# Low halves of the later first-layer weight tiles on VectorE and GpSimd, with the planner's costs and offsets set anew, in a fused attention and feed-forward kernel

## Chip, cores and metric

The kernel runs on one core of a Trainium2 chip. A time is the device time of one execution in microseconds (us), and lower is better. The profile is of one execution of its own.

## What is computed

Block-sparse attention over 4 batches, 8 heads, 768 positions and head size 64, then a feed-forward layer with a leaky activation over all 3072 tokens:

```python
scores = scale * np.matmul(q, k.transpose(0, 1, 3, 2))
...
scores = np.where(mask, scores, -1000000000.0)
scores = scores - np.max(scores, axis=-1, keepdims=True)
attn = np.exp(scores)
attn = attn / (np.sum(attn, axis=-1, keepdims=True) + 1e-09)
return np.matmul(attn, v).astype(np.float32)
...
h = x @ w_in            # x: 3072 x 512, w_in: 512 x 2048
g = np.maximum(h, 0.0) + alpha * np.minimum(h, 0.0)
return (g @ w_out).astype(np.float32)
```

The two weight matrices arrive in eight bytes a number.

## The kernel before, in words

**Split numbers.** Every matmul runs in 16 bit. A number is split into a high part, which is the number scaled by a power of two and rounded to 16 bit, and a low part, which is what the rounding left out, and a product takes three matmuls: high with high, high with low, low with high. `times` makes a high part. `rest` makes a low part, with one instruction on VectorE (DVE in the rows), and with two on GpSimd (POOL): a scaling (L443) and a subtraction (L444).

**Attention.** There are 48 units (a batch, a group of 256 query rows, a pair of heads) of four steps, 192 steps in all. Two steps share one group of eight score matmuls (L653, L659). Per step VectorE adds the mask (`emit_bias`, L669), ScalarE (ACT) takes the exponential (L676), a reciprocal follows (L687), then the high part on ScalarE, GpSimd or VectorE and the low part on VectorE or GpSimd. A DMA from SyncE's queue transposes the pair (`pt<-ph`). When a unit's four steps are there, 36 matmuls multiply by v (L730), and `x` is made, its high part by ScalarE (L741) and its low part by VectorE (L746).

**Feed-forward.** Four units make a chunk of 256 tokens, 12 chunks in all. Per chunk there are eight ups (`emit_up`, 24 matmuls, L1149) and eight downs (`emit_down`, 12 matmuls, L1191). Between up and down, VectorE makes `g` in two instructions (L1159, L1160), ScalarE its high part (L1165) and GpSimd its low part (`emit_gl`, L1170). In a chunk the downs run two ups behind.

**Weights.** There are 16 tiles of `w_in` (`wi` in the rows) and 16 of `w_out` (`wo`), each 512 columns on 128 partitions. After its load a tile goes through three integer steps (L930, L935 or L940, L946), a matmul that finds its scale (`emit_gram`), a high part (`times`), and a low part. For all 16 `wi` tiles and the first 8 `wo` tiles, the low part goes through TensorE (PE): a scaled identity `sid` is made on GpSimd (L1022 or L1026), one 32-bit matmul of the tile with `sid` (L1033, two rows in the trace) and one 16-bit matmul that takes the high part away (L1034) leave the low part in PSUM, and ScalarE copies it to its place (L1038). The last 8 `wo` tiles have their low part made by `rest` on VectorE. The first up stands behind the last scale (`emit_gsc`) in the order.

**What sets the order.** `Plan.run` works through all operations once, before the program is built. It keeps a clock and the queue of each engine; an operation has a priority, a table of engines with a cost on each (`alts`), the operations it needs and the buffers it takes. The constants at the head of the file (`V_WA`, `OFF`, `PREF`, `MOE_LAG`, `MOE_BOOST` and others) set priorities and how dear each engine counts. The result is one fixed order of instructions on each engine, and on the chip each engine goes through its own in that order.

```python
o = plan.op(p + 0.1 + OFF["wh"], {"ACT": 0.63, "DVE": (0.42, 0), "POOL": 0.75}, lambda e, y=y: emit_w_hi(e, "wi", y), [gs[-1], prev])
db = plan.buf("o")
o = plan.op(p - 2 + OFF["wl"], {"PE": 1.2}, lambda y=y, db=db: emit_w_lo_pe("wi", y, db), [o, o_sid], [db], [sb])
prev = o_wi[y] = plan.op(p + OFF["wc"], {"ACT": 0.5}, lambda y=y: emit_w_lo_copy("wi", y), [o], [], [db])
```

## Time and profile before

| | |
|---|---|
| three runs | 816.24, 816.78, 818.37 us, median 816.78 us |
| the profiled execution | 818.19 us, of which the span from the first to the last instruction is 816.5 us |
| busy, share of the span | TensorE 96%, weight loads 62%, VectorE 74%, ScalarE 71%, GpSimd 53% |
| instructions | 16929 |
| DMA | 135.35 MB, mean 166 GB/s |
| first up starts | 115.15 us after the start of the span |

A table of busy shares is a mean over stages. In the span cut into 40 slices the first five look unlike the rest, so the profile is read in two stretches, before and behind the first up. A chain of waits says what the end waited for, and a table of waits in a stretch says what an engine waited for there.

### The profile page before, as it was taken

To read this page: it belongs to the slowest core of one execution; us is meant where nothing else is said; L and a number is where in the kernel's file an instruction comes from. 1 tells how busy PE (TensorE), PEld (TensorE's weight loads), DVE (VectorE), ACT (ScalarE), POOL (GpSimd) and SP (SyncE) were. 2 spreads that over 40 slices of the span, in tenths; PEclk is the share of its full clock that TensorE was granted. 3 is DMA by queue.
4 is the path that set the end of the run, shared out by engine and by line. 5 is a ranking of instruction groups with operands and counts; after the bars stand their busy time and mean duration, and the time that the engine had idled before them with its cause. 6 is when DMAs were issued, how large, how long until landed. Compare 5 with 4: busy or idle time off the path is not lost.

```text
span 816.5 us, 16929 instructions
## 1 busy us (share of the span) xinstructions
PE 781.6 (96%) x6335; PEld 504.1 (62%) x6335; DVE 604.9 (74%) x1279; ACT 576.0 (71%) x1041; POOL 429.9 (53%) x360
## 2 busy tenths in 40 slices
PE   6848899999999999999999999999999999999997
PEld 4423365766766666666666666666666666676764
DVE  6898998887689777797687787958687888734231
ACT  6888997897577778876677878736587888724111
POOL 6475786575336555644355655544265656624121
PEclk9978999999999999999999999999999999999999
DMA  9997996987985979879787979629686887643000
GB/s 331 325 310 208 191 184 146 205 161 162 220 193 122 169 162 194 183 153 199 160 174 142 183 179 209 136 77 193 154 204 157 171 171 151 115 97 84 28 1 26
DMA packets 384722, 135.35 MB, mean 166 GB/s; under 512 B 349028, under 2 KB 377728, under 8 KB 384640
## 3 DMA queue, kind: packets, MB, share of 16 engines
q1 hardware_dynamic: 384576, 134.26, 74.8%
q8 instruction: 49, 0.80, 0.4%
q14 instruction: 33, 0.27, 0.1%
q0 software_dynamic: 64, 0.02, 0.0%
HBM read 35.67 MB, written 6.29 MB: 51 GB/s over the span
## 4 chain that ended last, share of the span: by engine, by line
PE 87%; DVE 4%; ACT 3%; POOL 2%; issue 1%; DMA 1%; POOLq 0%; ACTq 0%; DVEq 0%
PE h L1149 30%; PE o L1191 29%; PE sp L730 12%; PE sp L653 7%; PE sp L659 5%; PE d L1033 3%; ACT wo L935 1%; DVE e L669 1%; DMA kf<-in_k_dram 1%; PE d L1034 1%; POOL ph L444 1%; DVE n L930 1%; PE gram L956 0%; DVE ph L441 0%; POOL e L443 0%
## 5 line engine op out<-in xcount | busy, mean ns | idle before, releaser
L1149 PE MATMUL h<-x,wi 128*128 128x256 f16 x2304 | 267.2, 273 | 0.0
L1149 PEld LDWEIGHTS <-wi 128*128 128x128 f16 x2304 | 222.1, 98 | 46.9 <-issue 10.1
L1170 POOL TENSOR_TENSOR gl<-g,gh 128x512 f16<-128x512 f32 x96 | 115.7, 1205 | 220.3 <-ACT gh L1165 192.2
L1191 PE MATMUL o<-wo,gh 128*128 128x512 f16 x768 | 228.9, 380 | 0.0
L669 DVE CUSTOM_DVE_ANT_0 e<-sp,bias,cs 128x768 f32<-128x768 f32 x192 | 191.2, 1010 | 34.7 <-PE sp L659 16.6
L676 ACT ACTIVATE e<-e,nm 128x768 f32<-128x768 f32 x192 | 177.4, 925 | 18.6 <-DVE nm L669 18.4
L444 POOL TENSOR_TENSOR ph<-e,ph 128x768 f16<-128x768 f32 x96 | 171.6, 1788 | 8.0
L433 ACT ACTIVATE ph<-e,rs 128x768 f16<-128x768 f32 x181 | 164.4, 926 | 10.2 <-DVE rs L687 4.9
L443 POOL TENSOR_SCALAR e<-e,rs 128x768 f32<-128x768 f32 x96 | 92.4, 962 | 112.4 <-ACT ph L433 104.9
L1165 ACT CAST gh<-g 128x512 f16<-128x512 f32 x96 | 59.1, 616 | 125.6 <-DVE g L1160 106.0
L1191 PE MATMUL o<-wo,gl 128*128 128x512 f16 x384 | 145.5, 379 | 0.3 <-POOL gl L1170 0.3
L1159 DVE SCALAR_TENSOR_TENSOR g<-h,am 128x512 f32<-128x512 f32 x96 | 66.1, 689 | 78.3 <-PE h L1149 72.2
L1191 PEld LDWEIGHTS <-gh 128*128 128x128 f16 x768 | 70.5, 98 | 82.2 <-issue 6.3
L441 DVE SCALAR_TENSOR_TENSOR ph<-e,rs,ph 128x768 f16<-128x768 f32 x96 | 111.8, 1164 | 8.9 <-ACT ph L433 8.8
L730 PE MATMUL sp<-pt,v 128*64 128x256 f16 x1728 | 103.5, 274 | 0.0
L730 PEld LDWEIGHTS <-v 128*64 128x64 f16 x1728 | 90.6, 110 | 15.7 <-issue 15.0
L1160 DVE SCALAR_TENSOR_TENSOR g<-h,gsc,g 128x512 f32<-128x512 f32 x96 | 72.1, 751 | 3.4
L1191 PEld LDWEIGHTS <-gl 128*128 128x128 f16 x384 | 37.5, 98 | 46.0 <-POOL gl L1170 0.8
L653 PEld LDWEIGHTS <-qt 128*128 128x128 f16 x384 | 37.6, 98 | 29.3 <-issue 7.5
L653 PE MATMUL sp<-kt,qt 128*128 128x512 f16 x192 | 47.5, 330 | 3.6 <-DVE nm L669 3.6
L741 ACT ACTIVATE x<-sp 128x256 f16<-128x256 f32 x48 | 18.3, 380 | 43.6 <-DVE nm L669 25.1
L659 PE MATMUL sp<-kt,qt 64*128 64x512 f16 x192 | 48.2, 332 | 0.0
(152 smaller groups left out, 725.7 us busy)
## 6 DMA issues: line engine op xcount, KB each, us to landing
wo<-in_moe_w_in_dram SPq DMA_DIRECT2D x16, 512.0 KB, 6.4
raw<-in_moe_w_out_dram SPq DMA_DIRECT2D x16, 512.0 KB, 6.6
kf<-in_k_dram SPq DMA_DIRECT2D x16, 384.0 KB, 3.9
qf<-in_q_dram SPq DMA_DIRECT2D x12, 512.0 KB, 4.8
vf<-in_v_dram SPq DMA_DIRECT2D x16, 384.0 KB, 5.3
out_dram<-ob SPq DMA_DIRECT2D x24, 256.0 KB, 2.3
ks<-kt SPq DMA_DIRECT2D x28, 192.0 KB, 3.3
pt<-ph SPq DMA_TRANSPOSE x192, 3.5
```

Source lines behind the costliest of these rows:

```text
L433: nc.scalar.activation(dst, src, AF.Copy, scale=scale)
L441: nc.vector.scalar_tensor_tensor(dst, src, scale, hi, ALU.mult, ALU.subtract)
L443: nc.gpsimd.tensor_scalar(tmp, src, scale, 1.0, ALU.mult, ALU.mult)
L444: nc.gpsimd.tensor_tensor(dst, tmp, hi, ALU.subtract)
L653: nc.tensor.matmul(T["sp", n + i][:, a:z], T["qt", u][:, h, i, :], (ks, kt)[i][:, h, a:z], start=True, stop=False)
L659: nc.tensor.matmul(T["sp", n + i][:, a:z], T["qt", u][r, h, i, :], (kt, ks)[i][r, h, a:z], start=False, stop=True)
L669: nc.vector.tensor_tensor_reduce(T["e", n], T["sp", n], bias[:, t0 + j % w, :], scale=T["cs", c][:, hp : hp + 1], scalar=3.0e38, op0=ALU.a ...
L676: nc.scalar.activation(T["e", n], T["e", n], AF.Exp, bias=T["nm", n], scale=-1.0, accum_out=T["su", n])
L730: nc.tensor.matmul(av[h * D : (h + 1) * D, : n * P], v2[:, h, t, vv, :], T["pt", u, h][:, pl * NT + t, :], start=(m == 0), stop=(m == len( ...
L1149: nc.tensor.matmul(ph[:, i, :], win(w, f, ct), x[:, ct, :], start=(m == 0), stop=(m == len(terms) - 1))
L1170: nc.gpsimd.tensor_tensor(T["gl", c, j], T["g", c, j], T["gh", c, j], ALU.subtract)
L1191: nc.tensor.matmul(T["o", c][t], g[:, i, t * P : (t + 1) * P], wout(w, f), start=(i == 0 and m == 0 and j in first_j), stop=(i == 1 and m ...
```

## The change

Of the 16 `wi` tiles, tiles 8 to 15 no longer have their low part made through TensorE. They use `rest`, on VectorE or GpSimd as the planner picks, and no `sid` is made for them. The last 8 `wo` tiles may now use GpSimd as well. Softmax steps before step 22 may all use either engine for the low part (`PL0`), where before every second one was held to VectorE. `pa` (a buffer unused here) is no longer kept apart. All other lines change the planner's costs, its offsets, and the time after which it takes a DMA to have been issued.

```diff
-MOE_LAG = 17.620982
+MOE_LAG = 10.557759
-MOE_BOOST = 22.980404
+MOE_BOOST = 59.091694
...
-PL0 = "dv"
+PL0 = "d"
...
+WI_PE = 8
...
-    MAX4 = {"DVE": (0.55, 0), "ACT": 0.88, "POOL": 0.95}
-    LOW4 = {"DVE": (0.94, 0), "POOL": (1.1, 1.7)}
+    MAX4 = {"DVE": (0.55, 0), "ACT": 0.88, "POOL": 0.92}
+    LOW4 = {"DVE": (0.96, 0), "POOL": (0.94, 1.52)}
+    LOWW = {"DVE": (0.67, 0), "POOL": (0.75, 1.24)}
...
         for g in (2 * x, 2 * x + 1):
             sb = plan.buf("sid")
-            o_sid = plan.op(p + OFF["wh"], {"POOL": 0.5}, lambda g=g: emit_sid(g), [gs[-1]], [sb])
+            if 2 * g < WI_PE:
+                o_sid = plan.op(p + OFF["wh"], {"POOL": 0.41}, lambda g=g: emit_sid(g), [gs[-1]], [sb])
             for y in (2 * g, 2 * g + 1):
...
+                if y >= WI_PE:
+                    prev = o_wi[y] = plan.op(p + OFF["wc"], LOWW, lambda e, y=y: emit_w_lo(e, "wi", y), [o])
+                    continue
                 db = plan.buf("o")
...
-            o_wo[y] = plan.op(p - 3 + 0.1 * (y % HF) + OFF["oh"], {"DVE": (0.67, 0)}, lambda e, y=y: emit_w_lo(e, "wo", y), [o])
+            o_wo[y] = plan.op(p - 3 + 0.1 * (y % HF) + OFF["oh"], LOWW, lambda e, y=y: emit_w_lo(e, "wo", y), [o])
```

Lines of the program behind the change are numbered two higher in the helpers and six higher in the feed-forward part. What the change moves is seen at two places.

**TensorE, just ahead of the first up.** `v` is the value tile of attention, `d` the PSUM tile of a weight tile's low part, `h` the result of an up. Before:

```order
L730 LDWEIGHTS v_710
L730 MATMUL sp_74<-pt,v_710 64x256
L1033 MATMUL d<-wi,sid 128x512
L1034 LDWEIGHTS wi
L1034 MATMUL d<-wi 128x512
L1149 LDWEIGHTS wi
L1149 MATMUL h<-x,wi 128x256
```

Of the change:

```order
L732 LDWEIGHTS v_858
L732 MATMUL sp_74<-pt,v_858 64x256
L1155 LDWEIGHTS wi
L1155 MATMUL h<-x,wi 128x256
L1155 LDWEIGHTS wi
```

The low part between the product with v and the first up is gone. Ahead of the first up stand in both orders 11 groups of scores, 4 products with v, the low parts of 8 `wo` tiles, and the low parts of 14 `wi` tiles before and of 8 in the change. Behind it stand the low parts of 2 `wi` tiles before and of none in the change; scores, products, ups and downs are the same in number.

**GpSimd, up to the first low part of `g`** (`gl`), which the first down waits for. `e` and `ph` belong to one softmax step, `qn` to the queries. Before:

```order
L1022 TENSOR_SCALAR sid_1418<-wi_75,ssc_117 128x128
L437 TENSOR_SCALAR wi_75<-wi_75,ssc_117 128x512
L443 TENSOR_SCALAR e_1360<-e_1360,rs_1395 128x768
L444 TENSOR_TENSOR ph_1416<-e_1360,ph_1416 128x768
L437 TENSOR_SCALAR wi_75<-wi_75,ssc_117 128x512
L437 TENSOR_SCALAR qn_1531<-qf_1365,sq_1517 128x8x2x64
L437 TENSOR_SCALAR wo_76<-wo_76,swo_125 128x512
L437 TENSOR_SCALAR ph_1588<-e_1479,rs_1555 128x768
L1170 TENSOR_TENSOR gl_1596<-g_1538,gh_1559 128x512
```

Of the change:

```order
L444 TENSOR_SCALAR wi_75<-wi_75,ssc_117 128x512
L445 TENSOR_TENSOR wi_75<-wi_75 128x512
L444 TENSOR_SCALAR e_1234<-e_1234,rs_1340 128x768
L445 TENSOR_TENSOR ph_1363<-e_1234,ph_1363 128x768
L444 TENSOR_SCALAR e_1326<-e_1326,rs_1373 128x768
L445 TENSOR_TENSOR ph_1389<-e_1326,ph_1389 128x768
L444 TENSOR_SCALAR wi_75<-wi_75,ssc_117 128x512
L445 TENSOR_TENSOR wi_75<-wi_75 128x512
L1176 TENSOR_TENSOR gl_1565<-g_1536,gh_1548 128x512
```

Scalings of single tiles have given way to pairs of a scaling and a subtraction. Four of the five weight tiles that GpSimd takes over, and 15 softmax low parts where there were 10, stand ahead of the first `gl`; the fifth stands between the second `gl` and the third. The three tiles that VectorE takes over stand on it behind the first up.

## Rows read from the trace of the kernel before

**Rows 1.** The page: its span, TensorE's line of the busy times, its line in the 40 slices (tenths busy), and the chain of waits that ended last, by engine.

```profile
span 816.5 us, 16929 instructions
PE 781.6 (96%) x6335; PEld 504.1 (62%) x6335; DVE 604.9 (74%) x1279; ACT 576.0 (71%) x1041; POOL 429.9 (53%) x360
PE   6848899999999999999999999999999999999997
PE 87%; DVE 4%; ACT 3%; POOL 2%; issue 1%; DMA 1%; POOLq 0%; ACTq 0%; DVEq 0%
```

**Rows 2.** Stretches of the span, from and to in us: length, busy us and instructions of each engine, TensorE's granted clock as a share of full speed, DMA share, GB/s. The cuts are GpSimd's first softmax low part, its first `gl`, and the first up.

```profile
0.00:38.30 38.30, 26.73 (x184) 16.43 (x186) 28.22 (x71) 27.68 (x35) 19.51 (x36) 0.96 1.04 324
38.30:121.10 82.80, 64.20 (x457) 34.09 (x454) 76.76 (x173) 75.15 (x130) 59.79 (x56) 0.88 0.97 232
0.00:115.15 115.15, 84.98 (x595) 46.38 (x595) 99.10 (x231) 96.89 (x151) 74.49 (x88) 0.90 0.99 265
115.15:816.50 701.35, 696.59 (x5742) 457.69 (x5740) 505.76 (x1049) 479.08 (x891) 355.45 (x273) 1.00 0.71 149
```

**Rows 3.** TensorE in order of time around the first up: start, length, line, output and inputs, shape, count.

```profile
113.97 1.12 PE L1033 MATMUL d<-wi,sid 128*128 128x512 f32 x2
...
115.15 2.78 PE L1149 MATMUL h<-x,wi 128*128 128x256 f16 x24
117.77 1.02 PE L1033 MATMUL d<-wi,sid 128*128 128x512 f32 x2
...
118.85 0.49 PE L653 MATMUL sp<-ks,qt 128*128 128x512 f16 x2
...
120.02 2.79 PE L1149 MATMUL h<-x,wi 128*128 128x256 f16 x24
122.65 1.02 PE L1033 MATMUL d<-wi,sid 128*128 128x512 f32 x2
...
123.73 0.49 PE L653 MATMUL sp<-ks,qt 128*128 128x512 f16 x2
```

**Rows 4.** Waits of TensorE's matmuls between the first up and 812.2 us, all of them: what waited, for what, us in total, how often, the longest.

```profile
PE o L1191 <- POOL gl L1170: 0.3, 1, 0.3
```

**Rows 5.** VectorE's instructions from the start to 121.2 us, some groups: line, operation, output and inputs, shape, count, busy us, mean ns of one, idle us before them and what ended it.

```profile
L669 DVE CUSTOM_DVE_ANT_0 e<-sp,bias,cs 128x768 f32<-128x768 f32 x23 | 23.2, 1010 | 3.2 <-PE sp L659 2.9 <-POOL ph L444 0.2
L441 DVE SCALAR_TENSOR_TENSOR ph<-e,rs,ph 128x768 f16<-128x768 f32 x10 | 10.7, 1072 | 0.1
L441 DVE SCALAR_TENSOR_TENSOR qn<-qf,sq,qn 128x512 f16<-128x512 f32 x5 | 4.2, 844 | 0.0
L940 DVE SCALAR_TENSOR_TENSOR n<-wo,n 128x512 int32<-128x512 int32 x4 | 2.7, 687 | 0.0
L435 DVE TENSOR_SCALAR v<-vf,sv 128x768 f16<-128x768 f32 x1 | 2.1, 2058 | 0.0
L441 DVE SCALAR_TENSOR_TENSOR kn<-kf,ks,kn 128x768 f16<-128x768 f32 x2 | 2.0, 1018 | 0.1
L963 DVE TENSOR_REDUCE isum<-gram 128x2 bf16<-128x256 f32 x4 | 1.7, 422 | 1.9 <-PE gram L956 1.8
L441 DVE SCALAR_TENSOR_TENSOR v<-vf,sv,v 128x768 f16<-128x768 f32 x1 | 1.7, 1655 | 0.0
L435 DVE TENSOR_SCALAR wo<-wo,swo 128x512 f16<-128x512 f32 x1 | 0.9, 892 | 0.0
L435 DVE TENSOR_SCALAR kn<-kf,ks 128x768 f16<-128x768 f32 x1 | 0.6, 620 | 0.0
L585 DVE COPY kt<-kp 128x768 f16<-128x768 f16 x1 | 0.6, 557 | 1.6 <-PE kp L574 1.6
L600 DVE COPY qt<-qp 128x512 f16<-128x512 f16 x1 | 0.4, 418 | 0.0
```

**Rows 6.** The same view for GpSimd.

```profile
L444 POOL TENSOR_TENSOR ph<-e,ph 128x768 f16<-128x768 f32 x10 | 17.1, 1707 | 0.8
L443 POOL TENSOR_SCALAR e<-e,rs 128x768 f32<-128x768 f32 x10 | 10.6, 1061 | 3.8 <-ACT ph L433 3.5
L437 POOL TENSOR_SCALAR ph<-e,rs 128x768 f16<-128x768 f32 x10 | 10.3, 1027 | 9.2 <-DVE rs L687 5.5 <-ACT dn L681 3.6
L437 POOL TENSOR_SCALAR wi<-wi,ssc 128x512 f16<-128x512 f32 x12 | 8.3, 694 | 9.5 <-PE d L1033 9.5
L444 POOL TENSOR_TENSOR v<-vf,v 128x768 f16<-128x768 f32 x3 | 4.9, 1648 | 0.3
L1022 POOL TENSOR_SCALAR sid<-wi,ssc 128x128 f32<-128x128 f32 x8 | 3.6, 456 | 7.8 <-PE d L1033 6.7 <-DVE ssc L424 1.0
L443 POOL TENSOR_SCALAR vf<-vf,sv 128x768 f32<-128x768 f32 x3 | 3.4, 1141 | 0.1
L437 POOL TENSOR_SCALAR qn<-qf,sq 128x1024 f16<-128x1024 f32 x1 | 1.6, 1552 | 1.1 <-DVE sq L424 1.1
L1170 POOL TENSOR_TENSOR gl<-g,gh 128x512 f16<-128x512 f32 x1 | 1.2, 1162 | 0.0
```

**Rows 7.** GpSimd in order of time: its first softmax low part, with the idle time ahead of it in brackets.

```profile
38.31 0.91 POOL L443 TENSOR_SCALAR e<-e,rs 128x768 f32<-128x768 f32 x1 [1.11 <-ACT ph L433]
39.31 1.65 POOL L444 TENSOR_TENSOR ph<-e,ph 128x768 f16<-128x768 f32 x1
```

More of the change, by code (lines that the diff above doesn't have):

```diff
@@ L27 @@
 SIZES0 = [2, 2, 2]
-MOE_LAG = 17.620982
+MOE_LAG = 10.557759
 EARLY = 15.72
-MOE_BOOST = 22.980404
-V_WA = -4.856569
-W_WA = 1.529176
-V_WB = 4.173325
-W_WB = 1.958978
-LDP = 19.4088
-PL_V = -11.034327
-P_V = 11.063658
+MOE_BOOST = 59.091694
+V_WA = -14.628893
+W_WA = 0.831846
+V_WB = -1.945082
+W_WB = 0.837098
+LDP = 9.849482
+PL_V = -30.458749
+P_V = 70.421934
 PL = "gv"
 NS0 = 22
-PL0 = "dv"
+PL0 = "d"
 LD = 6
@@ L47 @@
 LEADL = 2
-PREF = {"PE": 1.0, "DVE": 3.833567, "ACT": 1.034769, "POOL": 4.794428, "SP": 1.0}
-PREF0 = {"PE": 1.0, "DVE": 1.289575, "ACT": 0.2, "POOL": 0.2, "SP": 1.0}
-SLOW = 1.12
+PREF = {"PE": 1.0, "DVE": 5.665188, "ACT": 1.195828, "POOL": 9.828706, "SP": 1.0}
+PREF0 = {"PE": 1.0, "DVE": 1.638921, "ACT": 0.697709, "POOL": 0.2, "SP": 1.0}
+SLOW = 1.02
 UNTIL = 130.0
 SWITCH = 0.095
-JOIN = 59.615954
-OFF = {"k": -16.711194, "q": -6.049735, "s": -54.854228, "e": 27.549339, "p": -20.301281, "wg": -11.57007, "wh": 69.70885, "wl": -10.883701, "wc": 1.583105, "og": -6.200565, "oh": -4.877295, "ol": 49.769926, "t": 0.0}
-P_AV = 16.415788
+JOIN = 107.16054
+OFF = {"k": -29.572996, "q": -7.007518, "s": -43.09448, "e": 92.848819, "p": -2.021726, "wg": -59.516007, "wh": 83.953384, "wl": -13.645392, "wc": 7.750212, "og": -27.344996, "oh": 18.271827, "ol": 4.243761, "t": 0.0}
+P_AV = 11.44285
 Q_PE = 1
+WI_PE = 8
 N_PS = 6.0
@@ L63 @@
 M_PR = 0.0
-BUFS = {"wr": 4, "vf": 4, "qf": 1, "qt": 3, "qn": 1, "ph": 4, "e": 4, "pt": 4, "x": 2, "junk": 1, "sid": 2, "pa": 1, "kt": 4, "ks": 4, "v2": 4, "gh": 3, "gl": 3}
+BUFS = {"wr": 4, "vf": 4, "qf": 1, "qt": 3, "qn": 1, "ph": 4, "e": 4, "pt": 4, "x": 2, "junk": 1, "sid": 2, "kt": 4, "ks": 4, "v2": 4, "gh": 3, "gl": 3}
 class Buf:
@@ L72, with __init__ @@
 class Op:
-    def __init__(self, n, prio, alts, fn, deps, alloc, use, dma, mode, clear):
-        self.clear = clear
+    def __init__(self, n, prio, alts, fn, deps, alloc, use, dma, mode, clear, lead):
+        self.clear, self.lead = clear, lead
         self.n, self.prio, self.alts, self.fn, self.dma, self.mode = n, prio, alts, fn, dma, mode
@@ L95, in buf, with op @@
         return Buf(pools)
-    def op(self, prio, alts, fn, deps=(), alloc=(), use=(), dma=None, mode=(0, 0), clear=()):
-        o = Op(len(self.ops), prio, alts, fn, deps, list(alloc), list(use), dma, mode, clear)
+    def op(self, prio, alts, fn, deps=(), alloc=(), use=(), dma=None, mode=(0, 0), clear=(), lead=None):
+        o = Op(len(self.ops), prio, alts, fn, deps, list(alloc), list(use), dma, mode, clear, lead)
         for b in o.alloc + o.use:
@@ L210, in run @@
                     if o.dma is not None:
-                        events.append((now + c + 1.0, o.n, "dma", o))
+                        events.append((now + (c + 1.0 if o.lead is None else o.lead), o.n, "dma", o))
                     else:
@@ L860, in attend @@
         hi = plan.op(at("p") - 1, MAX4, lambda e: emit_p_hi(e, n), [o], [pb], [eb])
-        lo = LOW4 if path == "d" else {"POOL": (1.1, 1.7)} if path in "gG" else {"DVE": (0.94, 0)}
+        lo = LOW4 if path == "d" else {"POOL": LOW4["POOL"]} if path in "gG" else {"DVE": LOW4["DVE"]}
         lo = plan.op(at("p") - 1, lo, lambda e: emit_p_lo(e, n), [hi], [], [pb, eb])
         if path in "gvd":
-            o_pt[n] = [plan.op(n - 1, {"SP": 1.7}, lambda: emit_p_t(n), [lo], [ptbuf[u, h]], [pb], dma=1.75)]
+            o_pt[n] = [plan.op(n - 1, {"SP": 1.46}, lambda: emit_p_t(n), [lo], [ptbuf[u, h]], [pb], dma=1.75, lead=0.8)]
             return
@@ L1120, in prep_wo @@
         for y in range(x * HF, (x + 1) * HF):
-            o = plan.op(p - 3 + 0.1 * (y % HF) + OFF["oh"], {"ACT": 0.63, "DVE": (0.42, 0), "POOL": 0.75}, lambda e, y=y: emit_w_hi(e, "wo", y), [o_swo[x], o_wo.get(y - 1)])
+            o = plan.op(p - 3 + 0.1 * (y % HF) + OFF["oh"], {"ACT": 0.68, "DVE": (0.42, 0), "POOL": 0.62}, lambda e, y=y: emit_w_hi(e, "wo", y), [o_swo[x], o_wo.get(y - 1)])
             if WO_PE > x:
@@ L1242, in moe @@
         downs, pas = [], []
-        obufs, pbufs = None, [plan.buf("pa") for _ in range(n)] if half else []
+        obufs, pbufs = None, [plan.buf("vf") for _ in range(n)] if half else []
         for i, (kind, j) in enumerate(items):
```

22 lines of the change are left out of this document (11 added, 11 removed).

## Prediction

> **What bounds the kernel.** I read the page first. TensorE is busy for 96% of the span, the chain of waits that ended last is TensorE for 87%, and the slices show it at 9 from the sixth to the last but one, with fuller engines only ahead of that [rows 1]. A mean over such a span hides two stages, so I then cut it into stretches [rows 2]. Behind the first up, at 115.15 us, TensorE is busy for 696.59 of 701.35 us at the full clock, and the table of waits has one wait of its matmuls in all that time, 0.3 us on GpSimd's `gl` [rows 4]. There the time is the sum of TensorE's work and no other engine counts, so long as it keeps up. Ahead of the first up TensorE is busy for only 84.98 of 115.15 us [rows 2]; VectorE is busy for 99.10 and ScalarE for 96.89, and the DMA engines' share is 0.99. Nobody is alone the bound there. VectorE is nearest, and every step of softmax and every weight tile passes through it.
>
> So the time is the start of the first up plus what TensorE has to do behind it. The order has the same scores, products, ups and downs behind the first up in both versions, down to the same last run of ups and downs. The question is when the first up starts, and whether anything makes TensorE wait soon after.
>
> **Term 1: TensorE's work behind the first up.** Two low parts of `wi` tiles go. One takes 1.08 us from its start to that of what follows (117.77 to 118.85 and 122.65 to 123.73) [rows 3]. The gain is 2 x 1.08 = 2.2 us, all of it on the path. With it the stretch of 701.3 us becomes 699.1. The six other low parts that go stand ahead of the first up, where TensorE idles for 30 us anyway; I count nothing for them. Their cover is VectorE's queue. If TensorE were what the first up waits for, they would give another 6 x 1.18 = 7.1 us [rows 3].
>
> **Term 2: the start of the first up.** The low part of `x` (L746) that completes the first chunk's input is the last thing VectorE owes the first up, so I compare what stands on VectorE up to there, with means from its rows [rows 5]. Less: five softmax low parts (5 x 1.07 = 5.4), two low parts of q (2 x 0.84 = 1.7), one mask step (1.1 with its accumulator), two copies of transposed tiles (0.56 + 0.42), one scaling of v against one low part of v (2.06 - 1.66 = 0.4). More: three integer steps (3 x 0.69 = 2.1), three softmax high parts (as the scaling of k, 3 x 0.62 = 1.9), one weight scaling more on balance (0.89) and four tiny ones (0.6). That is 9.6 less and 5.5 more, a gain of 4.1 us. The three `wi` low parts on VectorE come behind the first up, where it is busy for 505.76 of 701.35 us [rows 2], and cost nothing. ScalarE loses five copies from PSUM, five softmax high parts and three integer steps ahead of the first up and gains a handful of copies, so it has more room. Loads and transposes are the same in number on SyncE's queue, in another order; their share of 0.99 [rows 2] is a rival below.
>
> VectorE idles for 115.15 - 99.10 = 16.05 us ahead of the first up. If it idles as long again, the first up starts at 115.15 - 4.1 = 111.05 us. It could idle less: 2.9 us for scores, 1.8 for the scale sums and 1.6 for a copy that leaves it were waits for TensorE [rows 5], 6.3 us in all. That is the lower end, 104.75 us. The upper end is 115.15 us, nothing gained.
>
> **Term 3: GpSimd, and the first down.** The work that VectorE and ScalarE lose goes to GpSimd. Up to the first `gl` it has [rows 6]: five softmax low parts more (5 x (1.06 + 1.71) = 13.8), two softmax high parts (2.1), one scaling of q (1.6), four low parts of weight tiles and two of q; and less: seven weight scalings (7 x 0.69 = 4.9), four `sid` (1.8), one low part of v (2.8). No row has a low part 512 wide on GpSimd. Its two instructions are bounded below by the scaling of a tile and `gl`, the same widths, 0.69 + 1.16 = 1.86 us, and above by the pair 768 wide, 2.77 us. I take 1.86, since work here goes with width (0.69 against 1.03 us for scalings): 6 x 1.86 = 11.2. The sum is 28.7 - 9.5 = 19.2 us more.
>
> Before, GpSimd works 19.51 + 59.79 = 79.3 us until its first `gl`, and 98.5 us now. Its first softmax low part starts at 38.31 us [rows 7], with 19.5 us done by then. If that is so again, 79.0 us are left and the first `gl` starts at 117.3 at the earliest and ends at 118.5 us. TensorE comes to the first down three ups and one group of scores behind the first up, 2.62 + 2.63 + 2.63 + 1.17 = 9.05 us [rows 3], at 120.1 us. GpSimd may idle for 1.6 us in 79 without harm. Before it idled for 23 us in that stretch; many of those waits were for `sid` and scalings whose tiles TensorE still held (9.5 + 6.7 us in all [rows 6]) and mostly go. The waits for softmax, 5.5 + 3.6 + 3.5 = 12.6 us [rows 6], came to a queue that ran ahead of its inputs; it now runs behind them. I take 3 us of idleness, a quarter, since fewer arrivals should be late for a fuller queue, and keep 0 and 12.6 as ends. The first down then waits 3.0 - 1.6 = 1.4 us. The second `gl` is one softmax low part later, 2.77 + 1.16 us, while TensorE needs over 5 us to the second down, so no more waits follow.
>
> **The sum.** -2.2 - 4.1 + 1.4 = -4.9 us. The profiled execution took 818.19 us for a span of 816.5, so it would take 813.3. It is 1.4 us above the median of the runs; from 816.78 I get **811.9 us**. The ends: with a first up at 104.75 and GpSimd never idle, the first down still waits for the `gl` that ends at 118.5, as if the first up were at 109.45. That is -2.2 - 5.7 = -7.9, or 808.9. If GpSimd's scalings also keep to the 0.91 us of a single one [rows 7], 27 of them save about 4 us more, 805.
>
> **Rivals.**
>
> *The start gives more (0.20).* VectorE's waits for TensorE shrink, and GpSimd is never late: 805 to 809 us, by the ends above. For it: TensorE loses six low parts and ScalarE much work ahead of the first up. Against: GpSimd caps it.
>
> *The start gives nothing (0.17).* The first up waits for the stream of loads and transposes (DMA share 0.99 [rows 2]) or for ScalarE's chain, and starts at 115.15 again. Only term 1 is left: 816.78 - 2.2 = 814.6 us. Against: no group of VectorE's rows has a DMA as the end of its waits [rows 5].
>
> *GpSimd becomes the bound (0.10, slower).* If all 12.6 us of softmax waits stay, its first `gl` ends at 131.1 and the first down waits 11.0 us: -2.2 - 4.1 + 11.0 = +4.7, 821.5 us. It decides at the first down: from a wait of 6.3 us on the change loses. For it: GpSimd has to be busy for 79 of some 80 us, where it was busy for 59.79 of 82.80 [rows 2].
>
> *VectorE and GpSimd stand in each other's way (0.07, slower).* The scaling of v on VectorE took 2.06 us, that of k, the same shape, 0.62; the low part of v took 1.66 and that of k 1.02 [rows 5]. On GpSimd softmax scalings average 1.06 where a single one takes 0.91 [rows 6, 7]. VectorE has 16 scalings and low parts between tiles in SBUF ahead of the first up. If each is stretched by the 0.64 us of the low part of v, the first up starts 10.2 us later, at 121.3, and the time is 816.78 - 2.2 - 4.1 + 10.2 = 820.7 us. Against: the ten softmax low parts average 1.07, hardly over 1.02 [rows 5]. [...]
>
> That the change does not do what it says is ruled out by the order: the eight low parts are gone from TensorE.
>
> **How the numbers follow.** My forecast has 0.46, at 809 to 814 us. A change within 0.3% (2.4 us) can't be told from none, so faster means below 814.3 and slower above 819.2. Faster holds the forecast and the first rival, and a little of the second: 0.68. Same holds most of the second and the weak ends of the slower two: 0.18. Slower: 0.14. The range leaves out the slower cases' upper parts and the best of the first rival: 804.5 to 819.
>
> **What would show it.** Right: the first up near 111 us, 88 to 98 us of GpSimd's work done by its first `gl`, the stretch behind the first up near 699 to 701 us with one wait of 1 to 2 us at the first down. Wrong: a wait for `gl` of over 6 us or a first up behind 115 us (the slower cases), or TensorE waits spread over the later chunks, which would mean that the new offsets starve it and term 1's stretch is not the same work at the same pace.

## The result and the profile after

The changed kernel takes 821.91 us (median of six runs, 819.91 to 823.54) against 816.59 for the kernel before. The ratio is 1.0057, with a 95% interval from 1.0045 to 1.007: slower by 5 us. The prediction said 811.9 (804.5 to 819.0), faster. It was wrong in sign. The profiled execution took 823.54 us for a span of 821.8, 5.3 us more than the 816.5 of [rows 1]; both profiled executions, 823.54 and 818.19 us, stand 1.6 us above their medians.

A line of the page, as in [rows 1]:

```profile
PE 776.4 (94%) x6311; PEld 502.7 (61%) x6311; DVE 609.6 (74%) x1267; ACT 574.0 (70%) x1046; POOL 453.4 (55%) x374
```

TensorE's busy time is 5.2 us shorter than before, yet the span is 5.3 us longer: its idle time grew by 10.5 us. Stretches of the span: ahead of the first up and behind it as in [rows 2], up to GpSimd's first `gl`, from 95 to 130 and to 400 us, and two short ones (length, busy us of PE, weight loads, VectorE, ScalarE and GpSimd, granted clock, DMA share, GB/s):

```profile
0.00:112.12 112.12, 79.28 (x577) 43.94 (x577) 95.56 (x221) 86.37 (x137) 87.55 (x98) 0.82 0.98 268
112.12:821.80 709.68, 697.10 (x5737) 458.73 (x5735) 514.07 (x1047) 487.58 (x911) 365.88 (x277) 1.00 0.72 148
0.00:122.27 122.27, 86.36 (x636) 49.36 (x637) 105.50 (x242) 92.67 (x149) 96.20 (x105) 0.83 0.96 254
95.00:130.00 35.00, 28.44 (x257) 19.00 (x257) 32.41 (x72) 27.83 (x55) 31.07 (x29) 0.95 0.64 130
130.00:400.00 270.00, 264.55 (x2199) 172.64 (x2194) 218.58 (x437) 209.88 (x399) 148.43 (x109) 0.99 0.86 174
104.20:107.40 3.20, 3.20 (x34) 2.50 (x29) 1.85 (x7) 1.85 (x4) 2.92 (x4) 0.50 1.06 232
172.50:175.70 3.20, 3.20 (x33) 2.69 (x29) 0.00 (x0) 0.00 (x0) 1.39 (x2) 0.50 1.10 246
```

The same two stretches of the kernel before:

```profile
95.00:130.00 35.00, 33.72 (x285) 20.44 (x283) 31.97 (x80) 31.70 (x61) 28.04 (x26) 1.00 0.88 172
130.00:400.00 270.00, 270.00 (x2261) 177.95 (x2260) 212.69 (x447) 208.09 (x390) 141.84 (x108) 1.00 0.86 178
```

Length less busy time is TensorE's idle time: from 95 to 400 us 1.28 us before, 6.56 + 5.45 after, 10.7 more. What TensorE waited for behind 100 us in the changed kernel (us in total, how often, the longest); [rows 4], which begins at the first up, has a single 0.3, and 8.4 of the 11.9 us here stand behind the first up:

```profile
PE sp L655 <- DVE nm L671: 4.2, 3, 2.8
PE sp L732 <- DMA pt<-ph: 3.1, 2, 2.4
PE h L1155 <- ACT x L743: 2.3, 1, 2.3
PE sp L655 <- DVE uq L422: 0.9, 1, 0.9
PE h L1155 <- DVE x L748: 0.7, 1, 0.7
PE otot L977 <- DVE osum L965: 0.7, 1, 0.7
```

Most of it is softmax and `x`: scores wait for VectorE's mask step (`nm`), products for the transposed softmax parts (`pt`), ups for `x`. TensorE in order of time around the first up (L1155), and at 172 us:

```profile
102.74 0.49 PE L655 MATMUL sp<-kt,qt 128*128 128x512 f16 x2 [2.80 <-DVE nm L671]
...
103.58 3.58 PE L732 MATMUL sp<-pt,v 128*64 128x256 f16 x36
...
110.03 2.16 PE L732 MATMUL sp<-pt,v 128*64 128x256 f16 x36
112.12 0.50 PE L1155 MATMUL h<-x,wi 128*128 128x256 f16 x3
114.94 0.60 PE L1155 MATMUL h<-x,wi 128*128 128x256 f16 x4 [2.32 <-ACT x L743]
116.28 4.64 PE L1155 MATMUL h<-x,wi 128*128 128x256 f16 x41 [0.74 <-DVE x L748]
...
172.17 3.82 PE L732 MATMUL sp<-pt,v 128*64 128x256 f16 x35 [2.35 <-DMA pt<-ph]
```

Two things are to be seen. The first up starts at 112.12 us, near the forecast, but runs three matmuls and then waits 2.32 + 0.74 us for `x`; 17 of its 24 matmuls run from 116.28 us on, so it ends about where it did before. And the 36 matmuls of a product take 2.16 us, but 3.58 and (35 of them) 3.82 us behind a wait of 2.8 and of 2.35 us. The two short stretches above show why: the granted clock is 0.50 there, where the kernel before has 1.00 from 95 to 400 us. That costs 1.4 + 1.7 = 3.1 us more. The sum closes: 10.7 of waits, 3.1 of clock, less eight low parts of 1.08 us [rows 3], is +5.2 us against a measured +5.3.

It also shows where the change loses. From 130 to 400 us it idles for 5.45 us (3.1 for `pt`, 1.4 for `nm`, 0.9 for a scale of the queries, `uq`), where the kernel before is busy for 270.00 of 270, and one product there costs 1.7 us more at the half clock. These 7.2 us are more than the whole loss of 5.3: at 130 us the changed kernel was still about 1.9 us ahead.

### The profile page after: what moved, and what is told of

It is laid out like the page before. It is cut to its first block, busy times and chain, and to the rows that moved or that the text cites. A ratio compares the mean times of both kernels' runs of the same rounds, so it can differ in the third digit from the quotient of the medians.

```text
span 821.8 us, 16881 instructions
## 1 busy us (share of the span) xinstructions
PE 776.4 (94%) x6311; PEld 502.7 (61%) x6311; DVE 609.6 (74%) x1267; ACT 574.0 (70%) x1046; POOL 453.4 (55%) x374
## 4 chain that ended last, share of the span: by engine, by line
PE 54%; DMA 1%; ACT 0%; DVE 0%; issue 0%; DVEq 0%
PE o L1197 21%; PE h L1155 20%; PE sp L732 7%; PE sp L655 4%; PE sp L661 3%; DMA pt<-ph 1%; ACT e L678 0%; ACT ph L434 0%; DVE ob L1212 0%; ACT v L434 0%; ACT dn L683 0%; PE bc L617 0%; PE tot L521 0%; DVEq L1212 0%
## 5 line engine op out<-in xcount | busy, mean ns | idle before, releaser
L1155 PE MATMUL h<-x,wi 128*128 128x256 f16 x2304 | 267.3, 273 | 3.1 <-ACT x L743 2.3
L1155 PEld LDWEIGHTS <-wi 128*128 128x128 f16 x2304 | 222.5, 98 | 48.5 <-issue 10.1
L671 DVE CUSTOM_DVE_ANT_0 e<-sp,bias,cs 128x768 f32<-128x768 f32 x192 | 191.6, 1009 | 36.4 <-PE sp L732 16.7
L1176 POOL TENSOR_TENSOR gl<-g,gh 128x512 f16<-128x512 f32 x96 | 117.8, 1227 | 179.7 <-ACT gh L1171 139.0
L445 POOL TENSOR_TENSOR ph<-e,ph 128x768 f16<-128x768 f32 x101 | 181.2, 1794 | 8.4
L444 POOL TENSOR_SCALAR e<-e,rs 128x768 f32<-128x768 f32 x101 | 97.8, 968 | 148.5 <-ACT ph L434 147.5
L434 ACT ACTIVATE ph<-e,rs 128x768 f16<-128x768 f32 x177 | 159.9, 925 | 15.2 <-DVE rs L689 6.5
L442 DVE SCALAR_TENSOR_TENSOR ph<-e,rs,ph 128x768 f16<-128x768 f32 x91 | 107.0, 1176 | 16.2 <-ACT ph L434 16.2
L732 PE MATMUL sp<-pt,v 128*64 128x256 f16 x1728 | 108.0, 280 | 3.1 <-DMA pt<-ph 3.1
L732 PEld LDWEIGHTS <-v 128*64 128x64 f16 x1728 | 93.4, 112 | 20.0 <-issue 15.4
L655 PE MATMUL sp<-ks,qt 128*128 128x512 f16 x192 | 47.9, 332 | 1.5 <-ACT qt L600 1.5
L661 PE MATMUL sp<-ks,qt 64*128 64x512 f16 x192 | 48.5, 333 | 0.0
```

Source lines behind the costliest of these rows:

```text
L434: nc.scalar.activation(dst, src, AF.Copy, scale=scale)
L442: nc.vector.scalar_tensor_tensor(dst, src, scale, hi, ALU.mult, ALU.subtract)
L444: nc.gpsimd.tensor_scalar(tmp, src, scale, 1.0, ALU.mult, ALU.mult)
L445: nc.gpsimd.tensor_tensor(dst, tmp, hi, ALU.subtract)
L655: nc.tensor.matmul(T["sp", n + i][:, a:z], T["qt", u][:, h, i, :], (ks, kt)[i][:, h, a:z], start=True, stop=False)
L661: nc.tensor.matmul(T["sp", n + i][:, a:z], T["qt", u][r, h, i, :], (kt, ks)[i][r, h, a:z], start=False, stop=True)
```

## The experiments

Two theories stood after the result. **Order theory**: the new constants starve the softmax. **Load theory**: VectorE and GpSimd, given the low parts, are late with the softmax wherever the order comes from. A third, the **filler theory**, came with the first results: ahead of about 125 us TensorE's low parts stood in waits for softmax, filled them, and kept the clock up. To keep the order still, most kernels below are the kernel before with its own order as the planner worked it out, in which only the named operations are exchanged. Ratios are to the kernel before in the same comparison, with 95% intervals.

| run | what | median us | ratio (interval) |
|---|---|---|---|
| path_old_order | old order, lows on GpSimd (5) and VectorE (3) | 820.96 | 1.005 (1.0037 to 1.0063) |
| path_replanned | same path, planned anew, old constants | 832.72 | 1.0186 (1.0169 to 1.0203) |
| old_constants | changed kernel, old constants | 826.79 | 1.0111 (1.0098 to 1.0125) |
| old_lag | changed kernel, old lag | 822.96 | 1.0062 (1.0049 to 1.0075) |
| low_dropped | old order, the eight lows left out | 819.29 | 1.0023 (1.0014 to 1.0032) |
| low_both | old order, lows on TensorE and on the others | 822.29 | 1.0059 (1.0046 to 1.0073) |
| low_all_pool | old order, all eight on GpSimd | 822.23 | 1.0056 (1.0044 to 1.0069) |
| low_all_dve | old order, all eight on VectorE | 824.86 | 1.0091 (1.0077 to 1.0104) |
| change_low_dropped | changed kernel, the eight lows left out | 821.95 | 1.0066 (1.0049 to 1.0084) |
| last_two_dropped | old order, the two behind the first up left out | 815.58 | 0.9978 (0.9965 to 0.999) |
| low_pe_twice | old order, TensorE does the eight twice | 825.46 | 1.0097 (1.0079 to 1.0114) |
| change_x_first | changed kernel, `x` earlier | 822.53 | 1.006 (1.0046 to 1.0074) |
| last_two_pool | old order, the last two on GpSimd | 816.99 | 0.9996 (0.9985 to 1.0007) |
| last_two_pool_late | the same, later | 817.38 | 1.0002 (0.9993 to 1.0011) |
| eight_pool_late | old order, eight on GpSimd, late | 834.91 | 1.0226 (1.0204 to 1.0247) |
| low_pe_only | old order, eight on TensorE, nobody reads them | 817.45 | 1.0005 (0.9996 to 1.0014) |

### The path alone, and the constants alone

```diff
 (before.py, path_old_order)
- lambda y=y, db=db: emit_w_lo_pe("wi", y, db)
+ lambda y=y, db=db: emit_w_lo_pe("wi", y, db) if y < 8 else None
- lambda y=y: emit_w_lo_copy("wi", y)
+ lambda y=y: emit_w_lo_copy("wi", y) if y < 8 else emit_w_lo("POOL" if y < 13 else "DVE", "wi", y)
 ...       # and emit_sid only for g < 4
```

> The kernel before with its own order of work, instruction by instruction, in which only the eight low parts of wi tiles 8 to 15 leave TensorE: five to GpSimd (two instructions each), three to VectorE, each where the copy from PSUM stood in the order. Their eight ScalarE copies and four scaled identities go. Order theory (the new constants starve the softmax, the path is good): 8 x 1.08 = 8.6 us leave TensorE, of which at least the two behind the first up (2.2 us) are a gain, and no TensorE waits of over 2 us in sum come behind the first up: 810 to 814.5 us. Load theory (VectorE and GpSimd, fuller and blocking each other, are late with softmax wherever the order comes from): TensorE waits of 5 us or more behind 100 us, 817 to 823 us.

Measured 820.96, +3.6 us by its comparison's medians. The order theory in its simple form falls: with no constant changed, the path alone loses most of what the change loses. One place of it, VectorE in order of time:

```profile
115.62 1.72 DVE L441 SCALAR_TENSOR_TENSOR wi<-wi,ssc 128x512 f16<-128x512 f32 x1
...
121.42 0.89 DVE L441 SCALAR_TENSOR_TENSOR wi<-wi,ssc 128x512 f16<-128x512 f32 x1
...
123.14 1.01 DVE L669 CUSTOM_DVE_ANT_0 e<-sp,bias,cs 128x768 f32<-128x768 f32 x1
```

Two low parts, 2.6 us (1.72 and 0.89; in the changed kernel one took 0.74 at 141.37 us, with GpSimd idle beside it), now stand ahead of a mask step. The scores behind it wait, on TensorE:

```profile
124.21 0.48 PE L653 MATMUL sp<-ks,qt 128*128 128x512 f16 x2 [2.24 <-DVE nm L669]
```

In this trace the two low parts that left TensorE here (2.2 us) came back as one wait of 2.24 us.

The same path, planned anew from the old numbers (`path_replanned` adds to the kernel before only the branch for `y >= WI_PE` and its costs `LOWW`):

> The kernel before with only the path of the low parts changed, and the order worked out anew from the old durations and the old constants (lag, offsets, priorities). Order theory: the softmax keeps its old lead over the ups, 810 to 816 us, under 2 us of TensorE waits behind the first up. Load theory: 817 to 823 us with waits on softmax (L655, L732 or their like) of 4 us or more behind the first up.

Measured 832.72: the old constants with the new path give an order whose first up starts at 128.8 us. This is outside both ranges: the load theory had the sign, and its size was short by 10 us.

```diff
 (after.py, old_constants: MOE_LAG, MOE_BOOST, V_*, W_*, LDP, PL_V, P_V, PL0, PREF, PREF0, SLOW, JOIN, OFF, P_AV)
- MOE_LAG = 10.557759
+ MOE_LAG = 17.620982
 ...
```

> The changed kernel, its new durations kept, with the old lag, boost, offsets, priorities and preferences. Order theory: most of the loss goes, 811 to 817 us, since attention has its old lead of 17.6 instead of 10.6 steps. If the new durations and not the constants are the harm, or by the load theory: 819 to 824 us.

Measured 826.79, above both ranges. Its first up starts at 119.0 us; TensorE's idle time from 130 to 400 us is 1.57 us, where the changed kernel has 5.45:

```profile
130.00:400.00 270.00, 268.43 (x2260) 176.29 (x2259) 220.58 (x463) 208.27 (x391) 141.35 (x109) 1.00 0.87 177
```

With this path the new constants are better than the old ones by 5 us: they bring the start of the first up 7 us forward and give part of that back as waits later.

For `old_lag`, `MOE_LAG` alone was put back.

> The changed kernel with one number put back: the lag of the first-layer and second-layer work behind attention, 17.62 for 10.56 steps. Order theory in its narrow form (the lag alone): the 5.4 us of TensorE waits from 139 to 371 us go, and with them the 1.7 us of the lower clock at 172 us, the start stays: 813 to 817 us. Load theory: VectorE is as full between 120 and 160 us as before (over 19 of 20 us), the waits stay or move, 819 to 824 us.

Measured 822.96, no gain in the median. The profiled execution took 820.04 us, 2.9 less than the median, and in it TensorE idles for 2.7 us from 130 to 400 us (busy for 267.28 of 270); the median did not follow. The lag alone does not bring the time back.

### What TensorE's work was worth

```diff
 (before.py, low_dropped)
- emit_w_lo_pe("wi", y, db)
+ emit_w_lo_pe("wi", y, db) if y < 8 else None
- emit_w_lo_copy("wi", y)
+ emit_w_lo_copy("wi", y) if y < 8 else None
+ f = f - 8 if hl and f >= 8 else f        # in win()
 ...       # and emit_sid only for 2 * g < 8
```

> The kernel before in its own order, in which the eight low parts of wi tiles 8 to 15 are not worked out at all, neither on TensorE nor elsewhere (the ups take the low parts of tiles 0 to 7 in their place, so these terms of the result are left out). It splits the loss of the path in the old order (+4.1 us by medians of one comparison, 820.96 against 817.4, nearer +3.5) in two. Load theory: without the load on VectorE and GpSimd the saving of TensorE shows, 808 to 812 us (8 x 1.08 = 8.6 us less work), and the load is worth 9 to 13 us. Filler theory (TensorE waits for softmax there, so that low parts on TensorE lie in gaps, keep it busy and its granted clock up): 814 to 818 us, with waits on L669 behind 95 us and a granted clock under 1.00 between 95 and 116 us.

Measured 819.29, slower than the kernel before by 0.23%, although 8.6 us of TensorE's work, eight copies and four scaled identities are gone and nothing was added. This is the main finding. It lies above both ranges, 1.3 us above the filler theory's. A stretch as above, a short one behind the wait, and TensorE in order of time where the third low part stood before:

```profile
95.00:130.00 35.00, 27.87 (x253) 18.01 (x253) 32.65 (x79) 27.73 (x53) 24.38 (x21) 0.95 0.85 162
102.20:105.40 3.20, 3.20 (x32) 2.48 (x29) 1.96 (x7) 1.60 (x7) 0.92 (x2) 0.50 1.36 207
```

```profile
100.58 0.48 PE L653 MATMUL sp<-kt,qt 128*128 128x512 f16 x2 [2.03 <-DVE nm L669]
...
101.43 3.45 PE L730 MATMUL sp<-pt,v 128*64 128x256 f16 x36
...
117.77 2.02 PE L1150 MATMUL h<-x,wi 128*128 128x256 f16 x17 [2.46 <-DVE x L746]
```

TensorE reaches the scores 2.5 us earlier than before, at 98.06 instead of 100.54 us, waits 2.03 us for VectorE's mask step, and goes on at 100.58, where the kernel before has the same matmuls at 100.98. Behind the wait the product takes 3.45 us instead of 2.16, at a granted clock of 0.50 from 102.2 to 105.4 us; over the 35 us the clock is 0.95, where it was 1.00. TensorE idles for 7.13 of these 35 us, and for 1.28 in the kernel before, where low parts keep it at work. Not every wait here is followed by a lower clock: behind the 2.46 us it is 1.00 (from 116 to 140 us).

The longest wait of this trace behind 95 us has another story. In the first up TensorE waits 2.46 us for `x`, whose low part stands on VectorE behind a softmax low part of 2.40 us. That softmax low part in this run, GpSimd beside it, and then the same two engines in the kernel before:

```profile
113.42 2.40 DVE L441 SCALAR_TENSOR_TENSOR ph<-e,rs,ph 128x768 f16<-128x768 f32 x1
```

```profile
113.36 1.65 POOL L444 TENSOR_TENSOR ph<-e,ph 128x768 f16<-128x768 f32 x1
```

```profile
112.22 1.01 DVE L441 SCALAR_TENSOR_TENSOR ph<-e,rs,ph 128x768 f16<-128x768 f32 x1
```

```profile
112.27 1.74 POOL L443 TENSOR_SCALAR e<-e,rs 128x768 f32<-128x768 f32 x1 [0.40 <-ACT ph L433]
```

Here VectorE began 0.06 us behind GpSimd's subtraction and was 1.4 us late; before, it began 0.05 us ahead of GpSimd's scaling, and GpSimd was the late one (1.74 us for 0.91). So the loss of this run has two parts, the waits and the half clock where low parts had been, and a meeting of VectorE and GpSimd that went the other way. No run sets them apart.

> The kernel before in its own order; TensorE works out the eight low parts of wi tiles 8 to 15 into PSUM as before, but no copy takes them from there (the ups take the low parts of tiles 0 to 7 in their place, so these terms are left out). Against the eight dropped (819.3) only TensorE's work is back, 8.6 us. Filler theory (it stands in waits, holds the clock, and its removal turns into waits and slow matmuls): 816 to 817.5 us, less than with the work dropped, no granted clock of 0.5 behind 95 us. If the kernel with the work dropped lost by the missing copies or by chance meetings of VectorE and GpSimd: 819 us or more.

`low_pe_only` keeps `emit_w_lo_pe` for all tiles and has the last two `+` lines of the diff above. Measured 817.45: work whose result nobody reads makes the kernel about 1.5 us faster than leaving it out (1.0005 against 1.0023, each against the kernel before in its own comparison; the two intervals just touch at 1.0014). Its clock is at 1.00 from 95 to 400 us, and up to 130 us TensorE idles for 1.08 us:

```profile
95.00:130.00 35.00, 33.92 (x287) 20.54 (x286) 31.57 (x80) 28.01 (x54) 26.88 (x24) 1.00 0.79 164
```

This rules out the missing copies as the loss. It does not rule out the meeting: the softmax low part ahead of `x` took 1.00 us in this trace, again ahead of GpSimd.

For `last_two_dropped`, the diff of `low_dropped` has 14 for the 8 in its first two conditions, and in `win()` the low parts of tiles 6 and 7 stand in for 14 and 15.

> The kernel before in its own order without the two low parts that stand behind the first up (wi tiles 14 and 15, 2 x 1.08 us on TensorE, two copies on ScalarE, one scaled identity; the ups take the low parts of tiles 6 and 7 in their place, so these terms are left out). The first term of the prediction (behind the first up the time is the sum of TensorE's work): 2.2 us less, a ratio to before of 0.997, 814 to 815.5 us. Softmax theory (up to some 125 us the scores come from VectorE and TensorE's low parts lie in waits): no gain, a ratio of 0.999 to 1.002, 816 to 818 us.

Measured 815.58, 1.7 us less (the interval is 0.8 to 2.9 us): the first term of the prediction, 2.2 us, is right for these two by themselves. Dropping all eight is 3.7 us slower than dropping two, so taking away the six ahead of the first up as well did harm: waits, half clock and the meeting together.

```diff
 (before.py, low_pe_twice)
+ for _ in range(2 if name == "wi" and f >= 8 else 1):
      nc.tensor.matmul(d, sid, w, start=True, stop=False)
      nc.tensor.matmul(d, nident, hi, start=False, stop=True)
```

> The kernel before in its own order, where TensorE works out each of the eight low parts of wi tiles 8 to 15 twice (8 x 1.08 = 8.6 us more, the result is the same). If TensorE bounds the kernel behind 97 us, as its slices of 9 say: the seven in that stretch show, +7 us, 823 to 826. If TensorE has slack there that low parts fill: less than 2 us, 816 to 819. In between: it is just balanced with the softmax, so that work added shows and work removed does not: 819 to 823.

Measured 825.46, +8.1 us: nearly all of the added 8.6 show. So work added to TensorE is paid, and work taken away is given back behind the first up (1.7 of 2.2 us) and not ahead of it, where TensorE then meets the softmax.

### What the load costs, and where

> The kernel before in its own order, with both paths: TensorE works the eight low parts out as before (into PSUM, from where no copy is made) and GpSimd and VectorE do them too (five and three). It adds the load alone to the kernel before. Load theory: before + 9 to 13 us, 826 to 830. Filler theory: TensorE has its filler and its clock, the load costs only where VectorE is full, so no more than 3 us over the path alone in the old order: 818 to 824.

Measured 822.29 (`low_both` is `path_old_order` with `emit_w_lo_pe` and `emit_sid` kept). With `low_pe_only`, `low_dropped` and `path_old_order` it makes a square; the ratios are shown, since the four medians come from three comparisons:

| | no load on VectorE and GpSimd | load there |
|---|---|---|
| TensorE keeps the work | 1.0005 | 1.0059 |
| TensorE without it | 1.0023 | 1.005 |

Of 817 us, the load costs 4.4 us beside TensorE's work and 2.2 without it. Taking the work off TensorE costs 1.5 us without the load; beside it the intervals overlap, and no difference is shown. Of the 4.4 us, 2.1 are waits of TensorE's own low parts for high parts that GpSimd or ScalarE made late (0.80, 0.46 and 0.85 us in the trace), which the other three do not have. The load theory's 9 to 13 us were too much; 822.29 is in the filler theory's range.

> The path alone in the old order with all eight low parts on GpSimd (8 x 1.85 = 14.8 us there, none on VectorE). If VectorE's own load is what hurts (three low parts took 4.3 us between 95 and 146 us): 817 to 819 us, 2 to 4 less than the 820.96 of the split. If it is the blocking between the two engines, or GpSimd's queue: 821 to 825.

> The path alone in the old order with all eight low parts on VectorE (8 x 0.74 = 5.9 us there if nothing blocks it, none on GpSimd). If VectorE's own load is what hurts: 823 to 826 us. If it is the blocking by GpSimd's subtractions (a low part of wi on VectorE took 1.42 us beside GpSimd, against 0.74 without): VectorE has 5.9 us of work in place of 4.3 and is blocked less: 818 to 821.

Measured 822.23 with all on GpSimd and 824.86 with all on VectorE (`emit_w_lo("POOL", ...)` or `("DVE", ...)` for every tile from 8 on). All on VectorE is worse than the split (1.005); all on GpSimd can't be told from it. VectorE is the dearer of the two, so its own load counts; GpSimd is not free either, since 1.0056 is above the 1.0023 of `low_dropped`.

> The kernel before in its own order; only the low parts of wi tiles 14 and 15, the two that TensorE works out behind the first up, go to GpSimd, where the copy from PSUM stood in the order. TensorE 2 x 1.08 us less, GpSimd 2 x 1.86 more and one scaled identity less, in front of the first gl. If these two are pure TensorE time (as with the two dropped, 0.998) and GpSimd has the room: 814 to 816 us. If the load makes gl or softmax late: 817 to 820 us, with waits for gl of over 1 us.

```diff
 (before.py, last_two_pool)
- emit_w_lo_copy("wi", y)
+ emit_w_lo_copy("wi", y) if y < 14 else emit_w_lo("POOL", "wi", y)      # and emit_w_lo_pe only for y < 14
```

Measured 816.99, no gain shown: the 1.7 us that are there when the work is left out do not show when GpSimd does it (the two intervals overlap a little, from 0.9985 to 0.999). Where they can go, in its trace, on VectorE, then on GpSimd, then on TensorE:

```profile
126.75 1.02 DVE L669 CUSTOM_DVE_ANT_0 e<-sp,bias,cs 128x768 f32<-128x768 f32 x1 [1.23 <-POOL ph L444]
...
128.23 0.42 DVE L746 SCALAR_TENSOR_TENSOR x<-sp,x 128x256 f16<-128x256 f32 x1 [0.45 <-ACT x L741]
```

```profile
122.24 1.86 POOL L1170 TENSOR_TENSOR gl<-g,gh 128x512 f16<-128x512 f32 x1
...
125.07 1.65 POOL L444 TENSOR_TENSOR ph<-e,ph 128x768 f16<-128x768 f32 x1
```

```profile
128.71 0.48 PE L653 MATMUL sp<-kt,qt 128*128 128x512 f16 x2 [1.05 <-DVE x L746]
```

GpSimd, put back by the low part of tile 14 ahead of these lines and by a `gl` of 1.86 us (1.16 in [rows 6]), ends a softmax low part at 126.7 us. VectorE's mask step waits 1.23 us for that buffer `e`. The low part of `x` stands behind the mask step in VectorE's queue, and the scores wait 1.05 us for `x`.

> As the two last low parts on GpSimd, but later: that of tile 14 just ahead of the fourth up, that of tile 15 (and the high part of 15) just ahead of the fifth; the up that reads them is the eighth. GpSimd has 8 of 20 us free from 140 to 160 us in the kernel before. If the place of the load decides: 813.5 to 815.5 us, a ratio of 0.996 to 0.999, faster than the kernel before. If blocking of VectorE costs wherever it stands: 816 to 818 us.

Measured 817.38 (`order.insert(order.index(ups[y - 11]), o)` for the two and the high part of tile 15): no gain either. TensorE now waits 1.28 us for `x` at 148.8 us. VectorE, and GpSimd beside it, just ahead of that:

```profile
144.87 2.09 DVE L441 SCALAR_TENSOR_TENSOR wo<-wo,swo 128x512 f16<-128x512 f32 x1
```

```profile
144.77 1.64 POOL L444 TENSOR_TENSOR ph<-e,ph 128x768 f16<-128x768 f32 x1
```

A `wo` low part, 0.76 us on average in the kernel before, takes 2.09 us on VectorE beside GpSimd's subtraction. The mask step behind it is late, then `x`. A later place did not bring the gain back.

> The kernel before in its own order with all eight low parts on GpSimd, each pair (and the high parts chained between them) just ahead of the up three before the one that reads it, so all of them behind the first up. If the load costs by its place (ahead of and around the first up): as with the eight dropped, 818.5 to 820 us. If it costs by its amount: as with all on GpSimd in the old place, 821.5 to 823 us. If TensorE's work ahead of the first up were worth anything after all: 811 to 815 us.

Measured 834.91, worse than every expectation, by a wait that the experiment made itself. A low part is written over part of its tile's raw numbers and the next tile's high part over the rest, so high and low parts follow one another in a chain. ScalarE, in order of time:

```profile
163.49 0.72 ACT L433 ACTIVATE wi<-wi,ssc 128x512 f16<-128x512 f32 x1 [8.79 <-POOL wi L444]
```

The high part of tile 15 waits 8.79 us for GpSimd's low part of tile 14, with the high part of `x` queued behind it, and TensorE's scores wait 8.7 us for `x`. The run says nothing on the load by itself.

### The changed kernel in its own order

```diff
 (after.py, change_low_dropped)
- prev = o_wi[y] = plan.op(p + OFF["wc"], LOWW, lambda e, y=y: emit_w_lo(e, "wi", y), [o])
+ prev = o_wi[y] = plan.op(p + OFF["wc"], LOWW, lambda e, y=y: None, [o])
+ f = f - 8 if hl and f >= 8 else f        # in win()
```

> The changed kernel in its own order, in which the eight low parts of wi tiles 8 to 15 are not worked out (the ups take the low parts of tiles 0 to 7 in their place, so these terms are left out). VectorE loses 3 instructions (3.3 us as traced), GpSimd 10 (5 x 1.86 = 9.3 us or more). If the load is what the change loses by: 816 to 819 us. If its order of work loses by itself: 820 to 823 us.

Measured 821.95, the same as with the low parts. In the change's own order the load is not what it loses by. Its stretches:

```profile
95.00:130.00 35.00, 27.39 (x213) 17.46 (x213) 29.64 (x67) 24.81 (x48) 18.67 (x18) 0.85 0.65 130
130.00:400.00 270.00, 266.63 (x2232) 174.23 (x2230) 216.90 (x437) 212.22 (x401) 145.90 (x109) 0.99 0.86 175
```

TensorE idles for 7.6 and 3.4 us, hardly less than with the load, and the clock is lower (0.85 against 0.95). So the changed order, without the eight on TensorE, loses by itself. Common to the traces of all kernels in which TensorE does not have the eight is that it idles for 3.4 to 7.5 of the 21 us from 95 to 116 us; in the kernel before it is 1.3.

```diff
 (after.py, change_x_first)
+ n = order.index(o_gsc)
+ at = next(i for i in range(n, n + 40) if order[i].eng == "DVE" and order[i] is not o_gsc)
+ order[at:at] = [xh, xl]        # taken out of their places before
```

> The changed kernel, in which the high part of x of the first chunk's last unit is put ahead of one softmax high part in ScalarE's queue, and its low part right behind the scales in VectorE's. The first up should then run through at about 114 instead of 116.3 us. If TensorE's work behind it bounds: 2 us less, 819 to 820.5 us. If the softmax on VectorE bounds what follows: 821 to 823 us, with the 2 us back as waits of the score groups behind it.

Measured 822.53. The first up's waits fell from 3.06 to 0.68 us, and the scores behind it wait in their place:

```profile
113.95 4.64 PE L1155 MATMUL h<-x,wi 128*128 128x256 f16 x41 [0.68 <-DVE x L748]
...
120.20 0.48 PE L655 MATMUL sp<-kt,qt 128*128 128x512 f16 x2 [1.28 <-DVE nm L671]
```

The start of the first up was not what the time hung on.

## Why the prediction was wrong

**The view of what bounds the kernel** failed first. The prediction read 696.59 busy us of 701.35 and a single wait [rows 2, 4] as "the time is the sum of TensorE's work and no other engine counts, so long as it keeps up", and took from this that the stretch behind the first up would be 699.1 us. It was 709.68: TensorE idled for 12.6 us there, where it had idled for 4.8, and ran a product at half the clock. The other engines did not keep up in the new order; 7.2 us of the loss stand behind 130 us. In the old order too the sum was true for added work (+8.1 for 8.6 us) and false for removed work (+1.8 for -8.6): ahead of about 125 us the softmax over VectorE, ScalarE and GpSimd was close behind TensorE, and the low parts hid it.

**Term 1** (-2.2 us) was right in mechanism and size for the two low parts alone, in the old order: 1.7 us measured when they are left out. What failed is "cost nothing" for the work on the other engines: in the old order it cost 2.2 to 4.4 us, and only in the changed order did leaving it out gain nothing. The busy shares of 505.76 in 701.35 us [rows 2] were an average; in `last_two_pool` one softmax low part that came late on GpSimd, at 126.7 us, made TensorE wait.

"I count nothing for them", of the six ahead, was too kind: leaving them out as well costs 3.7 us in the old order, as waits, as half the clock and by one meeting of VectorE and GpSimd. Their cover was named as VectorE's queue; what was not asked is what TensorE does in their place.

**Term 2** (-4.1 us) was wrong in effect. The first up started at 112.12 us (forecast 111.05) and then waited to 116.28, so the near start is no success of the sum. The low part of `x` was named rightly as VectorE's last debt, but it was late: VectorE, then ScalarE, then GpSimd around it:

```profile
111.38 1.12 DVE L1002 TENSOR_SCALAR rg<-rg,s_wi 128x8 f32<-128x8 f32 x1
...
114.37 1.52 DVE L442 SCALAR_TENSOR_TENSOR ph<-e,rs,ph 128x768 f16<-128x768 f32 x1
115.81 0.41 DVE L748 SCALAR_TENSOR_TENSOR x<-sp,x 128x256 f16<-128x256 f32 x1
```

```profile
113.68 0.93 ACT L434 ACTIVATE ph<-e,rs 128x768 f16<-128x768 f32 x1 [1.46 <-DVE rs L689]
114.52 0.36 ACT L743 ACTIVATE x<-sp 128x256 f16<-128x256 f32 x1
```

```profile
111.31 1.16 POOL L445 TENSOR_TENSOR wi<-wi 128x512 f16<-128x512 f32 x1
```

VectorE's tiny steps of the scales were stretched beside GpSimd (the two longest 1.12 and 0.83 us, 0.54 and 0.17 before), the reciprocal `rs` behind them was late, ScalarE waited for it with the high part of `x` queued behind, and a softmax low part of 1.52 us (1.07 in [rows 5]) stood ahead of the low part.

VectorE did idle as long as supposed: when that low part ended, at 116.22 us, it had idled for 16.7 us (16.05 in the kernel before). What failed is the 4.1 us less of work: it had worked 99.48 us, against 99.23 at the same point before. The instructions that were to go had gone, but those left took longer: four softmax low parts 1.36 us each for the 1.07 of [rows 5], three softmax high parts 1.02 for the supposed 0.62, and the four steps that set the scales of `wi` 0.77 for 0.25 before. The three longest of these four (1.13, 0.91 and 0.72 us) each began inside a GpSimd subtraction and ended with it. And had `x` been early, the time would not have moved (`change_x_first`).

**Term 3** (+1.4 us) was right on GpSimd and needless on the path. It had 96.20 us of work done by its first `gl` (forecast 98.5), which ran from 122.27 to 123.43 us (forecast end 121.5), and the first down at 124.56 us did not wait for it, because TensorE was late too.

**The rivals.** "GpSimd becomes the bound" did not come at the first down. "VectorE and GpSimd stand in each other's way" has a part in it: the stretched instructions took the 4.1 us of term 2 back. But it did not come at its price, since the first up was not later than before. The case that came was the one in the last sentence of the prediction, waits spread over later chunks; it had no price and no chance, and should have had both.

What stays open: which of the new constants puts the waits of 5.45 us between 130 and 400 us. The old constants have 1.57 there, but start the ups 7 us later; the lag alone does not change the median; without the load 3.4 us stay. Open too is how much of the loss of `low_dropped` is the missing filler and how much the meeting. No version that computes everything was faster than the kernel before.

## What to carry to other kernels

TensorE was busy for over 9 tenths from 95 us on here and hardly waited. Work added to it showed nearly in full (+8.1 us for 8.6), but taking away the same work did not pay (+1.8 us for -8.6): ask what the second chain would let start earlier, and leave the work out in one run before it is moved elsewhere. Count a wait of TensorE twice where the trace shows a lower clock behind it: here three products behind waits of 2.0 to 2.8 us cost 1.3 to 1.7 us more each at 0.50, while behind the waits for `x` in the first up (2.32 + 0.74 us in the changed kernel, 2.46 in `low_dropped`) the clock stayed at 1.00. Price a moved instruction at the place in the queue where it lands, by who stands right behind it and by which engine it meets (a `wo` low part of 0.76 us took 2.09 beside GpSimd), and not by the engine's busy share.
